# Token numbers stored as three packets of 512 bytes; six raw chunks loaded ahead instead of four

## The chip, the cores and the metric

The kernel runs on one core of a Trainium2 chip. The metric is the device time of one execution, in microseconds (us). Engines: TensorE (PE: matmuls, PEld: weight loads), VectorE (DVE), ScalarE (ACT), GpSimd (POOL), and SyncE (SP), whose queue issues almost all DMAs here.

## The reference

Three stages follow each other. Attention over 2 batches, 8 heads, 768 positions and 64 columns a head, with a band of +-15 positions and 24 block summaries:

```python
mask_l = np.abs(pos[:, None] - pos[None, :]) < window          # window 16
scores_s = scale * np.einsum('bhsd,bhnd->bhsn', q, k_sum) + np.log(block)
a = softmax(concat([where(mask_l, scores_l, -1e9), scores_s]))
x = (a @ concat([v, v_sum])).transpose(0, 2, 1, 3).reshape(1536, 512)
```

A mixture of experts: 8 experts, each token goes to the one with the largest logit, if that one has fewer than 384 tokens yet:

```python
expert_idx = np.argmax(x @ w_gate, axis=1)
h = np.maximum(np.einsum('ecd,edf->ecf', disp, w1), 0.0)        # f = 1024
out[i] = gate_w[i] * y[expert_idx[i], pos[i]] if keep[i] else 0
```

And a dense layer with an ELU: `h = x @ w_in` (2048 columns), `g = where(h > 0, h, exp(min(h, 0)) - 1)`, `out = g @ w_out`. `w_in` and `w_out` come as float64.

## The kernel before

**Attention** runs tile by tile (12 tiles of 128 tokens, two groups of heads each). The gate of each tile finds its tokens' experts and places, and an indirect DMA writes each token's row to `xdisp` in device memory: 512 scaled values and the token's number (in columns 512 to 515).

**Units.** A unit is 384 rows of one expert. Its `load_rows` fetches the rows to `XROW` (128 partitions, 3 tokens in each), `split_x` transposes them and splits them into a high and a low part (`xh`, `xl`: the kernel multiplies float32 in three products), `layer1` and `layer2` are the expert's products, `evict` stores the result to `ydT`. The first unit (`first_unit`) is woven into the end of the attention by hand (`POINTS`, `fill_pe`); the others follow in nested branches, up to 12 in the program. With this input three units run: the first, unit 1 and unit 2 (16 activations of line 1119 are two units of eight). Then three **groups** of 384 rows go through the dense layer, and indirect DMAs write the output by the tokens' numbers.

**Token numbers.** The rows' numbers must come back at the end. `take_ids` (GpSimd) copies them from the rows to `IT`, one per partition and third; `put_ids` (SP, line 1044) stores `IT` to `ids` in device memory: 3 x 128 numbers, each 4 bytes from a partition of its own, thus 384 packets. `load_y` (line 1186) later loads 384 of them the other way, in packets of 4 bytes too.

**Raw chunks.** `w_in` and `w_out` are loaded as 32 chunks of 512 KB and converted from float64 to float32 by three VectorE instructions each (lines 390, 393, 384). Chunks 0 to 15 are `w_in`, 16 to 31 `w_out`. Four chunks (`AHEAD`, 8 to 11) are loaded near the end of the attention to rows 4 to 11 of `wout`, where its keys stood. The others share a ring of three buffers `RAW`: when chunk i of the ring has been converted, `conv_next` issues the load of the third one after it. Conversions 0 to 10 stand in the attention, 11 and 12 in the first unit, 13 to 20 in unit 1, 21 to 28 in unit 2, 29 to 31 in the first group. Rows 12 to 15 of `wout` hold two of the three `VXS` buffers (values of a tile) until the last tile.

**What sets the order.** The schedule is manual: each engine works through its instructions in the order written. SP's queue is in order too: a load that must wait for its buffer holds back all that are written behind it. All of SP's DMAs share one queue on 16 DMA engines.

Of the kernel before, what the change touches and what calls it, by code (L numbers as in the profile page):

```python
# [13 lines left out]
U32 = mybir.dt.uint32  # L14
# [37 lines left out]
def _consts():  # L52
    import numpy as np

    cols = []

    def add(name, a):
        full = np.zeros((P, a.shape[1]), np.float32)
        full[: a.shape[0]] = a
        CONST_COLS[name] = (sum(c.shape[1] for c in cols), a.shape[1])  # L60
        cols.append(full)

    p = np.arange(P)
    add("ident", np.eye(P, dtype=np.float32))
    q = p[:, None] % TQ
    n = np.arange(WK)[None, :]
    band = np.abs(n - WIN - q) < WIN
    first = band & (n >= WIN)
    last = band & (n < WIN + TQ)
    for name, ok in (("mid", band), ("first", first), ("last", last)):  # L70
        m = np.zeros((P, NK), np.float32)
        half = (p[:, None] < TQ) == (name == "first")
        m[:, :WK] = np.where(np.where(half, ok, band), 0.0, NEG)
        add(name, m)

    parts, rest = [], np.float32(8.0 * math.log(BLK))
    for _ in range(3):
        parts.append((np.array([rest]).view(np.uint32) & np.uint32(0xFFFF0000)).view(np.float32)[0])
        rest = np.float32(rest - parts[-1])
    m = np.zeros((P, NB), np.float32)  # L80
    for r in (0, D):
        m[r : r + 3] = np.array(parts, np.float32)[:, None]
    add("logs", m)
    m = np.zeros((P, NK), np.float32)
    m[p[: S // 8], WK + p[: S // 8] // (BLK // 8)] = 1.0 / BLK
    add("means", m)
    add("tri", (p[:, None] < p[None, :]).astype(np.float32))
    add("rev8", np.broadcast_to(E - np.arange(E, dtype=np.float32), (P, E)))
    u = np.arange(NU)
    e, c = u // NCH, u % NCH  # L90

    add("row0", np.repeat(p[:, None] == 0, NU, 1).astype(np.float32))
    add("e_row", np.broadcast_to(e.astype(np.float32), (NU, NU)))
    add("m_row", np.broadcast_to(-NCH * (e + 1.0), (NU, NU)).astype(np.float32))
    add("k_row", np.broadcast_to(NCH * e + 0.0, (NU, NU)).astype(np.float32))
    add("c_row", np.broadcast_to(c + 0.0, (NU, NU)).astype(np.float32))
    add("iota_u", np.broadcast_to(1 + np.arange(MAXU, dtype=np.float32), (NU, MAXU)))
    add("uconst", np.stack([SLOT * c, e, e * REG + SLOT * c - E * REG, e * REG, c >= 0, c == 0, SLOT * (c + 1), -NCH * (e + 1), NCH * e + c], 1).astype(np.float32))
    offsets = np.zeros((1, NLIST * MAXU), np.float32)
    offsets[:, MAXU : 2 * MAXU] = E * REG  # L100
    add("offsets", offsets)
    add("groups", SLOT * np.arange(NG, dtype=np.float32)[None, :])
    tok = (P * np.arange(NTT)[None, :] + p[:, None]).astype(np.int32)
    add("tok", tok.view(np.float32))
    fill = np.zeros((P, 4), np.int32)
    fill[:] = OOB
    add("oob", fill.view(np.float32))
    return np.ascontiguousarray(np.concatenate(cols, axis=1))


# [1 line left out]
def moe_chain_kernel(  # L112
# [83 lines left out]
    WA = [[wp.tile([P, KD, 2 * P], F32R, name=f"wa{w}{n}") for w in "hl"] for n in range(2)]  # L196
    WB = [[wp.tile([P, 2, DM], F32R, name=f"wb{w}{n}") for w in "hl"] for n in range(2)]
    HH = [[wp.tile([P, SLOT], F32R, name=f"h{w}{n}") for w in "hl"] for n in range(3)]
    IT = [cp.tile([P, NS], U32, name=f"it{n}") for n in range(2)]

    def load_w(e, parts, queue=nc.sync):
        for m in parts:
# [43 lines left out]
                )  # L246
            yield

    def split_x(xrow, hps):

        xh, xl = XS1
        for kk in range(KD):
            xp = hps[kk % len(hps)][:, 0:SLOT]
            for s in range(NS):
                nc.tensor.transpose(xp[:, s * P : (s + 1) * P], xrow[:, s, kk * P : (kk + 1) * P], ident)
            nc.scalar.copy(xh[:, kk, :], xp)
            nc.vector.tensor_tensor(xl[:, kk, :], xp, xh[:, kk, :].bitcast(F32), op=ALU.subtract)  # L257
            yield
# [24 lines left out]
    def first_unit():  # L283

        hps = [BANK[7], BANK[0]]
        yield from split_x(XROW0, hps)
        for f in range(F // P):
            hp = hps[f % 2][:, 0:SLOT]
            yield from layer1(hp, WA[f // 2 % 2], f % 2, XS1)
            nc.scalar.activation(HF0[f], hp, AF.Relu)  # L290
            if f % 2 and f // 2 + 2 < F // 256:
                split_a(f // 2 + 2, W1_RAW[f // 2 + 2])
            if f in B_AFTER:
                n = B_AFTER.index(f)
                split_b(WB[n], W2_RAW[n])
            if f in H_AFTER:
                n = H_AFTER.index(f)
                split_h(HH[n], n)
        yield "second"
        for f in range(NF1):  # L300
            yield from layer2(f, HH[f % 4], WB[f // 2 % 2])
            if f == 1:
                split_b(WB[0], W2_RAW[2])
            if f == 3:
                split_b(WB[1], W2_RAW[3])
            while len(HH) < 4:
                yield
            if f + 3 < NF1:
                split_h(HH[(f + 3) % 4], f + 3)
            held["f"] = f  # L310
# [35 lines left out]
    RAW = [wp.tile([P, CE], I64, name=f"raw{n}") for n in range(3)]  # L346


    AHEAD = range(8, 12)
    RING = [i for i in range(NCHUNK) if i not in AHEAD]  # L350

    def raw(i):
# [53 lines left out]
    with ExitStack() as att:  # L406
# [211 lines left out]
        def gate_3(i):  # L618
            gp = GPS[:, i % 2, :]
            lg = gp[:, 0:E]  # L620
            nc.tensor.transpose(lg, st.pop(("g2", i)), C("ident", E)[:, 0:E])
            xr = a3.tile([P, ROW], F32, tag="xr", name="xr")
            o, _ = CONST_COLS["tok"]
            nc.gpsimd.tensor_copy(
                xr[:, DM:].bitcast(U32), cst[:, o + i : o + i + 1].bitcast(U32).to_broadcast([P, ROW - DM])
            )
            mxl, r, nmx, s = sm("mxl"), sm("r") if i else r0, sm("nmx"), sm("s")
            vv, el = sm("vv", E), sm("el", E)
            nc.vector.tensor_reduce(mxl, lg, axis=AX.X, op=ALU.max)
            en = nc.vector if i >= last - 1 else nc.gpsimd  # L630
            en.tensor_scalar(nmx, mxl, -1.0, None, op0=ALU.mult)
            nc.vector.scalar_tensor_tensor(vv, lg, mxl, rev8, op0=ALU.is_ge, op1=ALU.mult)
            nc.vector.tensor_reduce(r, vv, axis=AX.X, op=ALU.max)
            oh = a2.tile([P, E], BF16, tag="oh", name="oh")
            nc.vector.tensor_scalar(oh, rev8, r, None, op0=ALU.is_equal)
            if i >= last - 1:
                nc.scalar.activation(el, lg, AF.Exp, bias=nmx, accum_out=s)
                st["g4", i] = (None, xr, s)
            if i == 0:
                ohs[0] = oh  # L640
            else:
                ohs[i] = oh_x if i == X_TILE else a3.tile([P, E], BF16, tag="ohsum", name="ohsum")
                en.tensor_tensor(ohs[i], ohs[i - 1], oh, op=ALU.add)
            st["g3", i] = (gp, oh, r, s, el, nmx, xr)
# [129 lines left out]
        def late(n):  # L774
# [10 lines left out]
                nc.vector.memset(ones_f, 1.0)  # L785
            if n == 1:
                nc.gpsimd.memset(fill_row, 0.0)
                nc.gpsimd.tensor_copy(fill_row[:, DM:].bitcast(U32), C("oob").bitcast(U32))
                nc.gpsimd.tensor_copy(oobs, C("oob")[:, 0:1].bitcast(U32).to_broadcast([P, REG // P]))  # L789
                nc.vector.tensor_copy(cap, cap_raw.bitcast(I32)[:, 0:1])  # L790
            if n in (2, 4):
                load_k(1, n - 2, 2)
# [34 lines left out]
                for m in range(len(RAW)):  # L827
                    conv_load(m)
            if n == NST - 2:
                for m in AHEAD:  # L830
                    conv_load(m)
            if n >= CONV_FROM and conv[0] < CONV_ATT and n % 2 == 0:
                pieces.extend(conversion(conv[0]))
# [82 lines left out]
        for gate, *at in tail:  # L916
            gate(*at)
            if gate is rest_o and at[1]:
                held["acc"] = False
            point()  # L920


# [114 lines left out]
    def expert_of(j, queue=nc.sync):  # L1037
        return queue.value_load(listed(0, j), min_val=0, max_val=E - 1)

    def take_ids(j, xrow):  # L1040
        nc.gpsimd.tensor_copy(IT[j % 2], xrow[:, :, DM].bitcast(U32))

    def put_ids(j, base, queue=nc.sync):
        queue.dma_start(ids[ds(base, SLOT), :].rearrange("(s p) o -> p s o", p=P), IT[j % 2].unsqueeze(2))

    def prologue(n):

        if n == 0:
            split_a(0, W1_RAW[0])
        elif n == 1:  # L1050
            for _ in split_x(XROW, HP):
                pass

    def branch_ahead(label, hint):
# [4 lines left out]
    def rest_of_first():  # L1059

        while not held["second"]:
            fill_pe(1)
        take_ids(0, XROW0)
        expert = expert_of(1)
        load_w(expert, range(2))
        load_x(1)
# [3 lines left out]
        while done < NF1 - 1:  # L1070

            while done < held["f"]:
# [3 lines left out]
                if done in CONV_FIRST:  # L1076
                    convert(CONVS[0] + CONV_FIRST.index(done))
                if done in PROLOGUE:
                    prologue(PROLOGUE.index(done))
                if done == HINT_FIRST:  # L1080
                    n_units = nc.values_load(listed(NLIST - 1, 0), min_val=0, max_val=MAXU)
                    branch_ahead("units0", n_units > 1)
# [14 lines left out]
    def unit(j, expert, finish):  # L1097

        if j > 1:
            load_w(expert, NEXT[2])  # L1100
            for n in range(2):
                prologue(n)
        base = nc.sync.value_load(listed(2, j), min_val=0, max_val=NT)
        if j + 1 < MAXU:
            branch_ahead(f"units{j}", n_units > j + 1)
        take_ids(j, XROW)
        put_ids(j, base)
        if j + 1 < MAXU:
            load_x(j + 1)
# [294 lines left out]
```

## Time and profile before

| | us |
|---|---|
| median of 3 runs | 448.73 (444.07, 448.73, 449.82) |
| the profiled execution | 448.12 |
| its span, first to last instruction | 446.4 |
| TensorE busy | 418.7 (94%) |
| VectorE busy | 344.6 (77%) |
| ScalarE busy | 234.0 (52%) |
| GpSimd busy | 71.0 (16%) |
| DMA queue of SP | 58.16 MB, 44.8% of 16 engines |

Up to 141 us attention and gate run, with parts of the first unit; the units to 235 us, the groups from there. The page cuts the span into 40 slices of 11.16 us; a digit is the busy share in tenths. The busy share of the whole span is a mean over stages with different limits; which engine another one waits for is read from the timelines of a stage. In a timeline a row gives start and duration, and in brackets the idle time of the engine before it with what ended that. `SPq` rows are issues of DMAs, not the transfers.

### The profile page before, as it was taken

Reading aid. Unit: us, or ns where it says so; the run is one execution under the profiler, and the core shown is the slowest. Engines: PE = TensorE matmul, PEld = TensorE weight load, DVE = VectorE, ACT = ScalarE, POOL = GpSimd, SP = SyncE. Lnnn points to the kernel's source line nnn. Section 1 sums busy time; section 2 is a strip of 40 time slices with the busy share of each in tenths; the row PEclk is TensorE's granted clock in tenths of the full one; section 3 lists DMA queues with packets and bytes.
Section 4 is the critical chain, followed back from the end, with each engine's and each line's share of the span. In section 5 each row is a group of like instructions: output and inputs, shape, how many; then the busy total and the mean of one; then the engine's idle time right before and its main releaser. Section 6 shows DMA issues by size and latency. Waiting matters only on the chain.

```text
span 446.4 us, 8022 instructions
## 1 busy us (share of the span) xinstructions
PE 418.7 (94%) x2759; PEld 360.5 (81%) x2759; DVE 344.6 (77%) x763; ACT 234.0 (52%) x581; POOL 71.0 (16%) x138
## 2 busy tenths in 40 slices
PE   7899999996887999789999999999999999999994
PEld 3567767774777999679998888788998988998983
DVE  4555998977675955979598999999777877777871
ACT  3364778884453565146347677754444334444331
POOL 2201685965311000000000000000200000200002
PEclk9967999998999999899999999999999999999999
DMA  8968799979501999889856900020100020100001
GB/s 271 245 183 270 249 322 287 282 220 292 214 0 34 188 288 204 280 277 147 310 187 220 346 6 1 0 73 0 72 1 1 0 71 1 71 1 0 1 3 71
DMA packets 33779, 63.50 MB, mean 142 GB/s; under 512 B 5877, under 2 KB 16117, under 8 KB 33728
## 3 DMA queue, kind: packets, MB, share of 16 engines
q1 hardware_dynamic: 32048, 58.16, 44.8%
q0 software_dynamic: 1680, 4.74, 2.8%
q8 instruction: 23, 0.38, 0.3%
q14 instruction: 28, 0.23, 0.2%
HBM read 50.26 MB, written 13.42 MB: 143 GB/s over the span
## 4 chain that ended last, share of the span: by engine, by line
PE 32%; issue 31%; DVE 19%; DMA 8%; ACT 5%; POOL 3%; SPq 1%; another core or an unknown queue 0%; POOLq 0%; DVEq 0%; ACTq 0%
PE bank L244 10%; PE bank L264 10%; PE bank L1232 3%; DMA raw<-in_moe_w_out_dram 3%; DMA w2raw<-in_v_dram 2%; PE bank L524 2%; PE bank L613 2%; DMA ydT<-ysb 2%; PE bank L576 2%; DMA cap_raw<-in_moe_capacity_dram 1%; DVE wout_r L1212 1%; PE bank L565 1%; DVE win_r L1212 1%; DVE mx L536 1%; POOL out_dram L1244 1%
## 5 line engine op out<-in xcount | busy, mean ns | idle before, releaser
L1232 PE MATMUL bank<-wout_r,hh 128*128 128x512 f32 x144 | 57.3, 398 | 1.5 <-DVE wout_r L1212 1.5
L548 ACT ACTIVATE ex<-bank,nm 128x120 f32<-128x120 f32 x96 | 33.6, 365 | 7.9 <-DVE nm L541 4.5
L1232 PEld LDWEIGHTS bank<-wout_r,hh 128*128 128x128 f32 x144 | 27.0, 188 | 7.3 <-DVE wout_r L1212 2.8
L1280 ACT ACTIVATE hf<-bank 128x384 f32<-128x384 f32 x24 | 11.8, 491 | 38.9 <-PE bank L244 38.9
L1280 ACT ACTIVATE xrow<-bank 128x384 f32<-128x384 f32 x24 | 11.8, 490 | 38.1 <-PE bank L244 38.1
L1232 PE MATMUL bank<-w2raw_r,hl 128*128 128x512 f32 x72 | 28.7, 399 | 0.0
L1232 PE MATMUL bank<-w2raw_r,hh 128*128 128x512 f32 x72 | 28.3, 393 | 0.0
L524 PE MATMUL bank<-spare,qt 64*64 64x120 f32 x384 | 26.7, 282 | 1.5 <-DMA qt<-in_q_dram 1.5
L244 PE MATMUL bank<-xh,wal 128*128 128x384 f32 x112 | 25.1, 346 | 3.1 <-DVE wal L237 3.1
L244 PE MATMUL bank<-yh,win_r 128*128 128x384 f32 x128 | 26.8, 337 | 0.0
L244 PE MATMUL bank<-xh,wah 128*128 128x384 f32 x112 | 24.6, 340 | 2.4 <-DVE xl L257 2.2
L1244 POOL DMA_INDIRECT out_dram<-raw,idt x6 | 6.1, 1023 | 119.8 <-ACT raw L1241 118.6
L244 PE MATMUL bank<-xl,wah 128*128 128x384 f32 x112 | 24.9, 344 | 0.0
L1244 POOL DMA_INDIRECT out_dram<-ysb,idt x3 | 2.9, 975 | 137.7 <-DVE xrow L1296 137.1
L524 PEld LDWEIGHTS bank<-spare,qt 64*64 64x64 f32 x384 | 21.0, 141 | 3.0 <-POOL oobs L789 1.2
L244 PEld LDWEIGHTS bank<-xh,wal 128*128 128x128 f32 x112 | 20.0, 192 | 3.9 <-DVE wal L237 3.4
L244 PEld LDWEIGHTS bank<-yh,win_r 128*128 128x128 f32 x128 | 22.7, 188 | 0.4
L244 PEld LDWEIGHTS bank<-xh,wah 128*128 128x128 f32 x112 | 19.7, 188 | 3.7 <-DVE xl L257 2.5
L1119 ACT ACTIVATE hf<-bank 128x384 f32<-128x384 f32 x16 | 7.9, 493 | 27.9 <-PE bank L244 27.7
L264 PE MATMUL bank<-hh,wbh 128*128 128x384 f32 x96 | 21.2, 343 | 0.0
L536 DVE TENSOR_REDUCE mx<-bank 128x4 f32<-128x480 f32 x24 | 15.6, 651 | 7.0 <-PE bank L524 6.9
L264 PE MATMUL bank<-hh,wbl 128*128 128x384 f32 x96 | 20.8, 337 | 0.0
(254 smaller groups left out, 1140.6 us busy)
## 6 DMA issues: line engine op xcount, KB each, us to landing
raw<-in_moe_w_out_dram SPq DMA_DIRECT2D x16, 512.0 KB
raw<-in_moe_w_in_dram SPq DMA_DIRECT2D x12, 512.0 KB
w1raw<-in_moe_w_dram SPq DMA_DIRECT2D x12, 512.0 KB
w2raw<-in_moe_w_dram SPq DMA_DIRECT2D x12, 512.0 KB
qt<-in_q_dram SPq DMA_DIRECT2D x12, 256.0 KB
w2raw<-in_v_dram SPq DMA_DIRECT2D x8, 384.0 KB
yr<-ydT SPq DMA_DIRECT2D x4, 768.0 KB
out_dram<-fill_row SPq DMA_DIRECT2D x4, 768.0 KB
```

Source lines behind the costliest of these rows:

```text
L244: nc.tensor.matmul(hp, wa[a][:, kk, cols], xa[b][:, kk, :], start=(n == kk == 0), stop=(n == 2 and kk == KD - 1))
L264: nc.tensor.matmul(ACC[d][:, 0:SLOT], wb[a][:, jj, d * P : (d + 1) * P], hb[b], start=(f == 0 and n == 0), stop=(f == NF1 - 1 and n == 2),)
L524: nc.tensor.matmul(sp[j * TQ : (j + 1) * TQ, u, :], qts[i][rows, u, j * TQ : (j + 1) * TQ], kws[i][rows, u, j, :], start=False, stop=(u == 3),
L536: nc.vector.tensor_reduce(mx, sp, axis=AX.X, op=ALU.max)
L548: nc.scalar.activation(ex[:, u, :], sp[:, u, :], AF.Exp, bias=nm[:, u : u + 1], scale=0.125, accum_out=den[:, u : u + 1])
L576: nc.tensor.matmul(op[j * TQ : (j + 1) * TQ, u, :], es[:, u, j * TQ : (j + 1) * TQ], vx[:, j, (2 * u + g) * D : (2 * u + g + 1) * D], star ...
L613: nc.tensor.matmul(lt, wg[:, kk, :], xT[:, kk, :], start=(kk == 0), stop=(kk == KD - 1))
L1119: nc.scalar.activation(hf, hp, AF.Relu)
L1212: nc.vector.tensor_tensor(lo, src, hi.bitcast(F32), op=ALU.subtract)
L1232: nc.tensor.matmul(ACC[s], ga[a][:, cols], wb[b][:, jj, :], start=(f == n == 0), stop=(f == NF2 - 1 and n == 2),)
L1244: put = nc.gpsimd.indirect_dma_start(out, bass.IndirectOffsetOnAxis(ap=IDT[g % 3][:, s : s + 1], axis=0), OBS[(NS * g + s) % len(OBS)], No ...
L1280: nc.scalar.activation(x, hp, AF.Relu, scale=-1.0)
```

## The change

Token numbers are float values now (`tok`, `oob`), no longer integer bits. `take_ids` on GpSimd is gone. Instead `split_x` begins with a product of the rows' number columns (128 x 3) with the identity, which gives 3 partitions of 128 numbers in a free part of a PSUM bank; ScalarE copies it to `IT`, now 3 x 128, as integers. `put_ids` stores it as three packets of 512 bytes. `AHEAD` holds six chunks: 8 to 11 are loaded where they were, 12 and 13 to rows 12 to 15 of `wout`, issued when the last tile's product with its values has been issued (`rest_o`). The ring loses chunks 12 and 13.

```diff
-    IT = [cp.tile([P, NS], U32, name=f"it{n}") for n in range(2)]
+    IT = [cp.tile([NS, P], U32, name=f"it{n}") for n in range(2)]
...
-    def split_x(xrow, hps):
+    def split_x(xrow, hps, it):
 
         xh, xl = XS1
+        at = hps[0][0:NS, SLOT : SLOT + P]
+        nc.tensor.matmul(at, xrow[:, :, DM], ident, start=True, stop=True)
+        nc.scalar.copy(IT[it], at)
         for kk in range(KD):
...
-    AHEAD = range(8, 12)
+    AHEAD = range(8, 14)
...
-                nc.gpsimd.tensor_copy(oobs, C("oob")[:, 0:1].bitcast(U32).to_broadcast([P, REG // P]))
+                nc.gpsimd.tensor_copy(oobs, C("oob")[:, 0:1].to_broadcast([P, REG // P]))
...
-                for m in AHEAD:
+                for m in AHEAD[:4]:
                     conv_load(m)
...
             if gate is rest_o and at[1]:
                 held["acc"] = False
+                for m in AHEAD[4:]:
+                    conv_load(m)
             point()
...
-    def take_ids(j, xrow):
-        nc.gpsimd.tensor_copy(IT[j % 2], xrow[:, :, DM].bitcast(U32))
-
     def put_ids(j, base, queue=nc.sync):
-        queue.dma_start(ids[ds(base, SLOT), :].rearrange("(s p) o -> p s o", p=P), IT[j % 2].unsqueeze(2))
+        queue.dma_start(ids[ds(base, SLOT), :].rearrange("(s p) o -> s (p o)", p=P), IT[j % 2])
```

SP's queue at the end of the attention, before and after (`rows` is `wout`, `raw_...` the ring; the order numbers the ring's buffers 154 to 156). Before:

```order
L365 DMA raw_154<-in_moe_w_in_dram 128x512
L365 DMA rows<-in_moe_w_in_dram 128x512 x4
L205 ISA
L205 DMA w2raw_136<-in_moe_w_dram 128x2x512
L365 DMA raw_155<-in_moe_w_in_dram 128x512
L1038 TENSOR_LOAD lists_i
```

After:

```order
L365 DMA raw_154<-in_moe_w_in_dram 128x512
L365 DMA rows<-in_moe_w_in_dram 128x512 x4
L202 ISA
L202 DMA w2raw_136<-in_moe_w_dram 128x2x512
L365 DMA raw_155<-in_moe_w_out_dram 128x512
L365 DMA rows<-in_moe_w_in_dram 128x512 x2
L1040 TENSOR_LOAD lists_i
```

The ring's load ahead of the lists was chunk 14 and is now chunk 16, of `w_out`; behind it stand the two new loads (chunks 12 and 13), still ahead of SP's read of the lists.

SP's queue in unit 1, from the store of the first unit's result to unit 2's first weights. Before:

```order
L1154 DMA ydT<-ysb 128x4x384
L365 DMA raw_154<-in_moe_w_out_dram 128x512
L365 DMA raw_155<-in_moe_w_out_dram 128x512
L365 DMA raw_156<-in_moe_w_out_dram 128x512
L365 DMA raw_154<-in_moe_w_out_dram 128x512
L1038 TENSOR_LOAD lists_i
L1038 ISA x2
L1136 TENSOR_LOAD lists_i
L1136 ISA x2
L1137 COMPARE_AND_BRANCH
L209 ISA
L209 DMA w1raw_122<-in_moe_w_dram 128x4x256
```

After:

```order
L1151 DMA ydT<-ysb 128x4x384
L365 DMA raw_156<-in_moe_w_out_dram 128x512
L365 DMA raw_154<-in_moe_w_out_dram 128x512
L365 DMA raw_155<-in_moe_w_out_dram 128x512
L1040 TENSOR_LOAD lists_i
L1040 ISA x2
L1133 TENSOR_LOAD lists_i
L1133 ISA x2
L1134 COMPARE_AND_BRANCH
L206 ISA
L206 DMA w1raw_122<-in_moe_w_dram 128x4x256
```

Four ring loads (chunks 16 to 19) stood ahead of unit 2's weights; now three (17 to 19). Chunk 20's load stands behind the first three weight loads in both.

ScalarE in the prologue of unit 1 (`xh` are the casts of `split_x`), after:

```order
L280 CAST hh_2208<-w1raw_128 128x384
L251 CAST it_153<-bank_92 3x128
L256 CAST xh_93<-bank_92 128x384
L256 CAST xh_93<-bank_85 128x384
L256 CAST xh_93<-bank_90 128x384
L256 CAST xh_93<-bank_91 128x384
```

Only the cast to `it` is new; the others stood in this order before. On TensorE the product stands likewise just ahead of the first transpose.

## Rows read from the trace of the kernel before

**Rows 1.** Page, 40 slices: TensorE's busy tenths, and GB/s of all DMAs

```profile
PE   7899999996887999789999999999999999999994
...
GB/s 271 245 183 270 249 322 287 282 220 292 214 0 34 188 288 204 280 277 147 310 187 220 346 6 1 0 73 0 72 1 1 0 71 1 71 1 0 1 3 71
```

**Rows 2.** Stages: length, busy us of each engine (instructions), granted clock, DMA share, GB/s

```profile
core 0: us, PE busy (x) PEld busy (x) DVE busy (x) ACT busy (x) POOL busy (x), PEclk, DMA share, GB/s
...
179.00:182.30 3.30, 0.18 (x2) 0.02 (x1) 3.02 (x5) 0.00 (x0) 0.00 (x0) 1.00 0.50 180
182.30:186.00 3.70, 3.70 (x12) 3.70 (x13) 3.63 (x6) 0.81 (x2) 0.00 (x0) 0.54 0.79 242
195.00:197.40 2.40, 0.17 (x2) 0.03 (x1) 2.40 (x5) 0.00 (x0) 0.00 (x0) 1.00 0.79 241
197.40:235.00 37.60, 37.60 (x216) 37.47 (x217) 30.53 (x48) 17.56 (x29) 0.00 (x0) 1.00 0.80 224
```

**Rows 3.** Timeline of TensorE: the two matmuls behind a gap, with what released them

```profile
182.28 1.56 PE L244 MATMUL bank<-xh,wal 128*128 128x384 f32 x4 [3.12 <-DVE wal L237]
...
197.37 0.98 PE L244 MATMUL bank<-xh,wah 128*128 128x384 f32 x4 [2.23 <-DVE xl L257]
```

**Rows 4.** Timeline of VectorE, units 1 and 2: first instructions of chunks 16, 17, 20, 24; `xl`

```profile
179.21 0.43 DVE L390 TENSOR_SCALAR wout<-raw 128x512 uint32<-128x512 uint32 x1 [5.53 <-DMA raw<-in_moe_w_out_dram]
...
182.61 0.42 DVE L390 TENSOR_SCALAR wout<-raw 128x512 uint32<-128x512 uint32 x1
...
191.76 0.43 DVE L390 TENSOR_SCALAR wout<-raw 128x512 uint32<-128x512 uint32 x1 [1.63 <-DMA raw<-in_moe_w_out_dram]
...
196.30 1.94 DVE L257 TENSOR_TENSOR xl<-bank,xh 128x384 fp32r<-128x384 f32 x4
...
217.64 0.43 DVE L390 TENSOR_SCALAR wout<-raw 128x512 uint32<-128x512 uint32 x1 [4.35 <-DMA raw<-in_moe_w_out_dram]
```

**Rows 5.** Stages of the DMA: around the stores of numbers, and two others

```profile
34.00:36.00 2.00, 2.00 (x19) 1.70 (x16) 0.31 (x1) 0.31 (x1) 0.00 (x0) 0.50 1.03 369
145.00:149.00 4.00, 4.00 (x24) 4.00 (x24) 3.93 (x7) 2.83 (x4) 0.00 (x0) 1.00 1.03 344
149.00:159.00 10.00, 10.00 (x63) 9.97 (x63) 7.15 (x12) 3.51 (x7) 0.35 (x1) 1.00 0.85 99
...
167.00:175.00 8.00, 8.00 (x48) 8.00 (x47) 6.55 (x10) 4.70 (x8) 0.00 (x0) 1.00 1.00 117
204.00:212.00 8.00, 8.00 (x48) 8.00 (x47) 7.19 (x13) 6.47 (x11) 0.00 (x0) 1.00 0.91 57
246.00:250.00 4.00, 4.00 (x22) 3.63 (x21) 3.86 (x8) 2.53 (x5) 0.00 (x0) 1.00 1.01 285
```

**Rows 6.** Timeline of SP: issues of stores to `ids`, a load from it, a ring load

```profile
29.42 0.38 SPq L794 DMA_DIRECT2D ids<-oobs  x1
...
115.71 0.33 SPq L365 DMA_DIRECT2D raw<-in_moe_w_in_dram  x1
...
147.20 0.41 SPq L1044 DMA_DIRECT2D ids<-it  x1
...
162.29 0.41 SPq L1044 DMA_DIRECT2D ids<-it  x1
...
201.99 0.41 SPq L1044 DMA_DIRECT2D ids<-it  x1
...
245.39 0.39 SPq L1186 DMA_DIRECT2D idt<-ids  x1
```

**Rows 7.** Chain of waits: chunk 16, start and length

```profile
167.83 11.28 DMA raw<-in_moe_w_out_dram
```

**Rows 8.** The ring's tile `raw`: its loads, from issue to landing

```profile
DMA to landing us min/median/max: 2.7/2.7/3.6
```

**Rows 9.** Timeline of TensorE: twelve transposes of unit 1

```profile
152.67 1.47 PE L255 MATMUL bank<-cst,xrow 128*128 128x128 f32 x12
```

**Rows 10.** Timeline of ScalarE: a small copy from PSUM

```profile
126.10 0.26 ACT L615 COPY ls<-bank 8x128 f32<-8x128 f32 x1 [0.82 <-PE bank L613]
```

More of the change, by code (lines that the diff above doesn't have):

```diff
@@ L102, in _consts @@
     add("groups", SLOT * np.arange(NG, dtype=np.float32)[None, :])
[L103 to L107, printed above, removed]
+    add("tok", (P * np.arange(NTT)[None, :] + p[:, None]).astype(np.float32))
+    add("oob", np.full((P, 4), OOB, np.float32))
     return np.ascontiguousarray(np.concatenate(cols, axis=1))
@@ L285, in first_unit @@
         hps = [BANK[7], BANK[0]]
-        yield from split_x(XROW0, hps)
+        yield from split_x(XROW0, hps, 0)
         for f in range(F // P):
@@ L624, in gate_3 @@
             nc.gpsimd.tensor_copy(
-                xr[:, DM:].bitcast(U32), cst[:, o + i : o + i + 1].bitcast(U32).to_broadcast([P, ROW - DM])
+                xr[:, DM:], cst[:, o + i : o + i + 1].to_broadcast([P, ROW - DM])
             )
@@ L787, in late @@
                 nc.gpsimd.memset(fill_row, 0.0)
-                nc.gpsimd.tensor_copy(fill_row[:, DM:].bitcast(U32), C("oob").bitcast(U32))
-                nc.gpsimd.tensor_copy(oobs, C("oob")[:, 0:1].bitcast(U32).to_broadcast([P, REG // P]))
+                nc.gpsimd.tensor_copy(fill_row[:, DM:], C("oob"))
+                nc.gpsimd.tensor_copy(oobs, C("oob")[:, 0:1].to_broadcast([P, REG // P]))
                 nc.vector.tensor_copy(cap, cap_raw.bitcast(I32)[:, 0:1])
@@ L1038, in expert_of, with prologue @@
         return queue.value_load(listed(0, j), min_val=0, max_val=E - 1)
-    def take_ids(j, xrow):
-        nc.gpsimd.tensor_copy(IT[j % 2], xrow[:, :, DM].bitcast(U32))
     def put_ids(j, base, queue=nc.sync):
-        queue.dma_start(ids[ds(base, SLOT), :].rearrange("(s p) o -> p s o", p=P), IT[j % 2].unsqueeze(2))
-    def prologue(n):
+        queue.dma_start(ids[ds(base, SLOT), :].rearrange("(s p) o -> s (p o)", p=P), IT[j % 2])
+    def prologue(j, n):
         if n == 0:
@@ L1050, in prologue @@
         elif n == 1:
-            for _ in split_x(XROW, HP):
+            for _ in split_x(XROW, HP, j % 2):
                 pass
@@ L1062, in rest_of_first @@
             fill_pe(1)
-        take_ids(0, XROW0)
         expert = expert_of(1)
@@ L1078, in rest_of_first @@
                 if done in PROLOGUE:
-                    prologue(PROLOGUE.index(done))
+                    prologue(1, PROLOGUE.index(done))
                 if done == HINT_FIRST:
@@ L1101, in unit @@
             for n in range(2):
-                prologue(n)
+                prologue(j, n)
         base = nc.sync.value_load(listed(2, j), min_val=0, max_val=NT)
@@ L1105, in unit @@
             branch_ahead(f"units{j}", n_units > j + 1)
-        take_ids(j, XROW)
         put_ids(j, base)
```

## The prediction

> **What bounds the kernel now.** I read the page's slices first [rows 1], 11.16 us each, counted from 0. From slice 13 (145 us) on TensorE is busy 90% or more, but for slices 16 and 17 (178.6 to 200.9 us: 0.7 and 0.8); and GB/s, which is near 280 around them, is only 188, 204 and 147 in slices 13, 15 and 18. So I asked for stages. [...]
>
> What ends the gaps? The first matmul behind the first one waited for `wal` of line 237, the one behind the second for `xl` of line 257, both VectorE's [rows 3]. On VectorE one reads why they were late [rows 4]: it sat 5.53 us until chunk 16, the first of `w_out`, had landed, and began its conversion at 179.21, ahead of `wal`. It waited once more, 1.63 us, for chunk 20, and `xl` began at 196.30. In unit 2 it waits a third time, 4.35 us, for chunk 24; there TensorE goes on without a gap [rows 2].
>
> Why is a load of 512 KB so slow? The DMA stages tell [rows 5]. After each of the three stores of token numbers (line 1044, issued at 147.20, 162.29 and 201.99 us [rows 6]) the engines stay 85 to 100% busy and yet move 99, 117 and 57 GB/s, for 10, 8 and 8 us, against 344 in the stretch ahead of the first. Such a store is 384 packets of 4 bytes. It is the store and not what comes with it: that stretch at 344 holds most of the first unit's `xrow` rows, which were issued ahead of the store; behind the 4-byte load of line 1186 (issued at 245.39) 285 are left; and the store of `oobs` (128 packets of 60 bytes, issued at 29.42) is followed by 369 at 34 to 36 us. Chunk 16 was issued at 167.83, behind the second store and three `xrow` loads, and stands with 11.28 us in the chain of waits [rows 7].
>
> **The change, part by part.** I count against the profiled execution: 448.12 us, its span 446.4, 0.6 under the median of the runs (448.73).
>
> (1) *The store becomes three packets of 512 bytes.* Before has none such. From below: the 60-byte packets cost nothing that is seen. From above: each packet at the price of a 4-byte one, 3/384 of 10 us, 0.1 us. I take 0; the slow stretches go.
>
> (2) *Chunks 12 and 13 go to places that the attention leaves.* The ring's chunks shift: where SP issued chunks 12, 13 and 14 it issues 14, 15 and 16. Chunk 15's and chunk 16's loads leave the busy time after 147 us, and two loads are added behind the last attention product. Chunk 16 takes the place of the load at 115.71 and has landed at 118.4, by the usual 2.7 us from issue to landing [rows 6, 8]. The two new loads run into a slice without bytes (slice 11, from 122.8 us: 0 GB/s [rows 1]), and their chunks are wanted in units 0 and 1, behind 145 us; without that cover they cost 2.7 us each. From chunk 17 on the loads run three ahead, as they did.
>
> (3) *What the vanished wait is worth.* VectorE is free at 179.21 - 5.53 = 173.68. Chunk 16 starts there: 5.5 us earlier. What is late next? Chunk 17, which VectorE reaches 3.4 us later (179.21 to 182.61 [rows 4]), at 177.1. Its load waits for the end of chunk 14, by that pace near 169 us; in an undisturbed queue it lands at 172. No wait; chunk 18 likewise. Chunk 19's load waits for the end of chunk 16, and behind it on SP stand unit 2's first weight loads and chunk 20's, as the rows of SP's order show: all of these move by the same 5.5 us, in the same order, so I keep chunk 20's wait of 1.63 us. Then `xl` starts at 190.8 instead of 196.30 and the matmul of 197.37 at 191.9. Is TensorE there by then? The product that it stood before at 182.28 follows at 178.99 (182.28 less 3.3, by the stage); up to that matmul there are 14 steps of four matmuls, 0.70 us each (216 in 37.6 us [rows 2]), the transposes (1.47) and the new product (0.1): 190.4. It still idles 1.5 us, and VectorE's chain is what counts: gain 5.5 us. What the low clock cost lies inside, since TensorE then waits anyway. Behind 197.4 TensorE is gapless, so the gain stays 5.5: the 4.35 us of chunk 24 are worth nothing more.
>
> (4) *The new product and copy.* One of each per unit, three units here. Transposes of the same 128 columns take 1.47 us for 12, 0.12 each; ScalarE's copy of 8x128 from PSUM 0.26 [rows 9, 10]. In the first unit both stand ahead of the first `xh`, on the way to an `xl` that the attention's own VectorE work queues behind: from 0 (ScalarE waits there) to 0.1 + 0.26. I take 0.3. In unit 1 (slices 13 to 15) TensorE is gapless: 0.1. In unit 2 both fall into its idle time: 0. GpSimd loses three copies that nothing waits for but the store; the store now waits for ScalarE's copy, next to the transposes at 152.67, and SP comes to it at 162.29: no new wait, and the loads queued behind it keep their places. `oobs` becomes a conversion on GpSimd, off every chain: 0.
>
> Sum: 448.12 - 5.5 + 0.3 + 0.1 = **443.0 us**, 1.3% under the median.
>
> **The rivals.**
> *Chunk 20 does not wait either.* With the queue clean its load may come the 1.6 us earlier; TensorE starts unit 2 at 190.4, when it can: 441.5. Against it: its queue mates move with it, and the second store was no longer in the way there. Chance 0.22.
> *The slow stretch stays* (it comes of storing to `ids` at all, or of the `xrow` loads). Then chunk 17 stands where chunk 16 stood and lands at 179.2; VectorE, there at 177.1, loses 2.1 of the 5.5: 448.12 - 3.4 + 0.4 = 445.1. Against it: the 60-byte store and the first `xrow` rows. 0.10.
> *The stall moves undiminished to chunk 17.* The ring still feeds it only three ahead. If it lands behind 177.1 + 5.5 = 182.6, nothing is gained, and product and copy are paid: 448.12 + 0.4 = 448.5, slower than before. For it: a load issued a little earlier took 11 us. Against it: even so, chunk 17 was converted at 182.61 without a wait [rows 4]. 0.08.
> *The clock falls in the gap that is left.* 3.3 us of idling were followed by 0.54 of the clock, 2.4 us were not [rows 2], so 1.5 us should not be. If it does, I take the stage from 182.3 to 186: 3.7 us at 0.54 do what 2.0 do at full clock, 1.7 lost: 444.7. [...] 0.08.
>
> **How the numbers follow.** My forecast has 0.52, the rivals in their order 0.22, 0.10, 0.08 and 0.08. From 440.0 to 446.5 lie all but the stall that moves, 0.92; I leave a tenth more at the edges for a median that is not the profiled execution (the three runs lie between 444.07 and 449.82). Two per cent, about what a measurement of this kernel can tell from no change, is 9.0 us. Faster than 439.8 is what the runs' spread makes of the first rival (a third of it) and of my own case (a tenth): 0.13. Slower than 457.7 is none of them; 0.03 for what I do not see. The rest, 0.84, is within 2%.
>
> **What would show it.** Right: no stretch under 200 GB/s behind a store of line 1043 while loads are pending; no VectorE wait for chunk 16; TensorE at full clock at 182 us and its first product of unit 2 near 191.9; two chunk loads in the slices that were empty. Wrong: VectorE waiting for chunk 17 or 18; TensorE idle longer than before ahead of 141 us; 57 to 117 GB/s behind the new stores; or a gain behind 197.4 us, where I expect none.

## The result and the profile after

| | us |
|---|---|
| kernel before, median of 20 runs | 449.68 (443.85 to 460.32) |
| changed kernel, median of 20 runs | 445.56 (439.59 to 453.34) |
| ratio changed / before, with its 95% interval | 0.9887 [0.985, 0.9924] |

The ratio is that of the faster executions of each kernel, so it is not the quotient of the two medians (0.9908). By the ratio the changed kernel takes 1.1% less: 5.1 us of 449.68, within two per cent. Put on the 448.12 us of the profiled execution before, that is 443.1, with an interval from 441.4 to 444.7; the forecast was 443.0, from 440.0 to 446.5. The lines below are from a second profile of the changed kernel (441.28 us, span 439.4), with a mean granted clock of 0.95 up to the routing (0.89 in the first).

The page's slices, 10.99 us each (TensorE's busy tenths, its granted clock in tenths, GB/s):

```profile
PE   7899899988987999999999999999999999999994
...
PEclk9999999995899999999999999999999999999999
...
GB/s 281 263 224 256 313 319 287 274 208 334 179 36 17 326 260 100 320 289 245 222 150 211 291 1 0 1 72 1 73 0 1 0 74 0 73 0 0 1 2 74
```

From slice 13 on TensorE is at 90% or more, but for the last slice: the 0.7 and 0.8 of slices 16 and 17 [rows 1] are gone, and slice 11, which was empty, carries bytes. The stages of the DMA tell more; the first three begin some 2 us behind each of the three stores:

```profile
147.00:155.00 8.00, 7.66 (x49) 7.11 (x48) 7.46 (x13) 3.76 (x8) 0.00 (x0) 1.00 1.00 321
157.00:165.00 8.00, 8.00 (x48) 8.00 (x47) 5.12 (x8) 5.67 (x9) 0.00 (x0) 1.00 0.71 218
197.00:205.00 8.00, 8.00 (x47) 8.00 (x47) 7.19 (x13) 6.27 (x11) 0.00 (x0) 1.00 0.75 205
190.65:192.65 2.00, 2.00 (x11) 2.00 (x12) 2.00 (x3) 0.00 (x0) 0.00 (x0) 1.00 0.99 297
```

321, 218 and 205 GB/s stand where 99, 117 and 57 stood [rows 5]. In the second and third the engines are only 71 and 75% busy: the queue is short of work there. The second pair does not compare like with like, since the stretch of [rows 5] began 5 us behind its store; from 2 us on, the kernel before moves 199 GB/s there. VectorE's timeline, the first instructions of chunks 16 and 17, then of chunk 20:

```profile
172.71 0.42 DVE L390 TENSOR_SCALAR wout<-raw 128x512 uint32<-128x512 uint32 x1
...
176.10 0.42 DVE L390 TENSOR_SCALAR wout<-raw 128x512 uint32<-128x512 uint32 x1
...
185.04 0.43 DVE L390 TENSOR_SCALAR wout<-raw 128x512 uint32<-128x512 uint32 x1 [1.41 <-DMA raw<-in_moe_w_out_dram]
```

Neither chunk 16 nor 17 is waited for; chunk 20 still is, 1.41 us after 1.63 [rows 4]. On TensorE the product that stood 3.12 us [rows 3] follows at once (178.12), and unit 2's first product stands 0.39 us instead of 2.23. What is new is a wait of the transposes:

```profile
178.12 0.85 PE L241 MATMUL bank<-xh,wal 128*128 128x384 f32 x4
...
185.89 0.38 PE L250 MATMUL bank<-cst,xrow 128*3 128x128 f32 x2
186.62 1.53 PE L255 MATMUL bank<-cst,xrow 128*128 128x128 f32 x12 [0.34 <-ACT it L251]
...
190.65 0.96 PE L241 MATMUL bank<-xh,wah 128*128 128x384 f32 x4 [0.39 <-DVE xl L257]
```

**A ruler.** Up to the routing the same program takes 140.8 to 149.9 us in the executions below, which is more than anything that is to be compared. The two extremes had a mean granted clock of 0.95 and 0.86 up to there; the clock is not all of it, since 140.98 and 144.60 us both stand at 0.93. So I measure from SP's first weight load of unit 1, issued right behind its read of the lists (142.60 before), to unit 2's first product, and on to the end of the span. In the timeline of SP, the kernel before:

```profile
142.60 0.40 SPq L209 DMA_DIRECT2D w1raw<-in_moe_w_dram  x1
```

and the changed kernel, with the loads of chunks 16, 12 and 13 ahead of it:

```profile
113.42 0.33 SPq L365 DMA_DIRECT2D raw<-in_moe_w_out_dram  x1
113.86 5.53 SPq L365 DMA_DIRECT2D rows<-in_moe_w_in_dram  x2
140.82 0.40 SPq L206 DMA_DIRECT2D w1raw<-in_moe_w_dram  x1
```

Each row is one profiled execution; (a) lists to unit 2's first product, (b) from there to the end, both in us:

| kernel | (a) | TensorE idle ahead of that product | (b) | (a)+(b) | ratio to before |
|---|---|---|---|---|---|
| before | 54.77 | 2.23 (and 3.12 earlier) | 249.03 | 303.80 | |
| changed | 49.83 | 0.39 | 248.75 | 298.58 | 0.9887 [0.985, 0.9924] |
| ids_only | 49.78 | 0.34 | 248.72 | 298.50 | 0.9822 [0.9778, 0.9867] |
| chunks_only | 50.47 | 2.83 | 250.49 | 300.96 | 0.9883 [0.9825, 0.9942] |
| pitch64 | 50.35 | 2.71 | 250.32 | 300.67 | 0.9881 [0.9797, 0.9965] |
| pitch64_chunks | 50.45 | 2.81 | 250.45 | 300.90 | none |
| bank_only | 49.51 | 0.75 | 248.74 | 298.25 | 0.9923 [0.987, 0.9977] |
| conv_later | 49.24 | none | 248.56 | 297.80 | 0.9833 [0.9788, 0.9879] |
| bank_conv | 48.58 | none | 248.62 | 297.20 | 0.9805 [0.9752, 0.9858] |
| pitch64_conv | 47.47 | none | 248.75 | 296.22 | 0.981 [0.9759, 0.9861] |
| pitch8 / pitch16 / wide32 | 49.99 / 49.64 / 50.13 | 2.37 / 2.00 / 2.49 | 250.17 / 250.42 / 250.38 | 300.16 / 300.06 / 300.51 | one run each |

Before to changed: 4.94 us in (a) and 0.28 in (b), 5.2 together, which the ratio's 5.1 agrees with. The first profile of the changed kernel gives 299.07. So differences of up to half a microsecond in this table are no more than the scatter of one kernel. Of the kernel before there is one profile. The ratios hardly separate the kernels of the table.

### The profile page after: what moved, and what is told of

Its sections match the earlier page's. It is cut to its first block, busy times and chain, and to the rows that moved or that the text cites. A ratio compares the mean times of both kernels' runs of the same rounds, so it can differ in the third digit from the quotient of the medians.

```text
span 444.5 us, 8028 instructions
## 1 busy us (share of the span) xinstructions
PE 423.7 (95%) x2765; PEld 363.9 (82%) x2765; DVE 346.6 (78%) x763; ACT 234.2 (53%) x584; POOL 69.2 (16%) x135
## 4 chain that ended last, share of the span: by engine, by line
PE 37%; issue 31%; DVE 14%; DMA 9%; ACT 4%; POOL 3%; SPq 1%; another core or an unknown queue 0%; POOLq 0%; DVEq 0%; ACTq 0%
PE bank L241 11%; PE bank L264 9%; PE bank L524 3%; PE bank L1229 3%; PE bank L576 2%; DMA raw<-in_moe_w_in_dram 2%; PE bank L565 2%; DMA w2raw<-in_v_dram 2%; PE bank L613 2%; DMA ydT<-ysb 2%; DMA raw<-in_moe_w_out_dram 2%; DVE wout_r L1209 1%; DVE win_r L1209 1%; DMA cap_raw<-in_moe_capacity_dram 1%; POOL out_dram L1241 1%
## 5 line engine op out<-in xcount | busy, mean ns | idle before, releaser
L1277 ACT ACTIVATE hf<-bank 128x384 f32<-128x384 f32 x24 | 11.8, 491 | 39.0 <-PE bank L241 39.0
L241 PE MATMUL bank<-xh,wah 128*128 128x384 f32 x112 | 25.7, 352 | 1.1 <-DVE xl L257 0.9
L264 PE MATMUL bank<-hl,wbh 128*128 128x384 f32 x96 | 20.6, 336 | 0.0
L1292 DVE SCALAR_TENSOR_TENSOR xrow<-hf,xrow 128x384 f32<-128x384 f32 x24 | 13.3, 556 | 9.3 <-ACT hf L1279 9.3
```

The costliest lines, as they stand in the source:

```text
L241: nc.tensor.matmul(hp, wa[a][:, kk, cols], xa[b][:, kk, :], start=(n == kk == 0), stop=(n == 2 and kk == KD - 1))
L264: nc.tensor.matmul(ACC[d][:, 0:SLOT], wb[a][:, jj, d * P : (d + 1) * P], hb[b], start=(f == 0 and n == 0), stop=(f == NF1 - 1 and n == 2),)
L1277: nc.scalar.activation(x, hp, AF.Relu, scale=-1.0)
L1292: nc.vector.scalar_tensor_tensor(z, x, 1.0, z, op0=ALU.add, op1=ALU.mult)
```

## The experiments

**The changed kernel again** (`again`).

> The changed kernel once more, for a profile of it at an undisturbed clock. My theory: TensorE has no gap near 182 us and full clock there; VectorE waits for no chunk up to 19, and 1.6 to 1.9 us for chunk 20; unit 2's first product comes near 191.9 us, 5.5 us earlier than before, and behind it nothing more is gained: about 443 us. Rival (the gain came from ahead of 145 us): the span from SP's read of the lists to the end is as long as before.

444.6 us, ratio 0.9899 [0.9827, 0.9972]. Its lines stand above: no gap near 182, chunk 20 waited for by 1.41 us, the first product 4.94 us earlier by the ruler. The rival falls: the gain lies behind the lists.

**The store alone** (`ids_only`).

```diff
-    AHEAD = range(8, 14)
+    AHEAD = range(8, 12)
```

> Only the store of three packets with its product and copy; four chunks ahead as before. My theory: the two parts of the change do the same work twice. With the queue clean, chunk 16, issued near 167.8 us as before, lands 3 to 4 us later, before VectorE comes to it at 173.7: no wait, no gap in TensorE, 448.1 - 5.5 + 0.4 = 443.0 us, as with the whole change. Rival A (the chunks that were moved carry the gain): VectorE still waits for chunk 16 by several us, about 448 us. Rival B (half and half): chunk 16 waits 2 to 3 us, about 445.5 us.

444.65 us. VectorE takes chunk 16 without a wait and waits 1.37 us for chunk 20; 298.50 us by the ruler against 298.58. The store by itself gives all that the ruler shows; the two chunks add nothing to it. Rivals A and B fall.

**The chunks alone** (`chunks_only`: the kernel before, with `AHEAD` as changed).

```diff
-    AHEAD = range(8, 12)
+    AHEAD = range(8, 14)
...
-                for m in AHEAD:
+                for m in AHEAD[:4]:
...
+                for m in AHEAD[4:]:
+                    conv_load(m)
```

> Only the six chunks; the store of 384 packets of 4 bytes stays. My theory: the stretches at 57 to 117 GB/s behind the stores stay; chunk 16 has long landed; chunk 17 stands where chunk 16 stood and lands near 179.2 us, VectorE is there at 177.1 and waits 2.1 us: 448.1 - 3.4 = 444.7 us. Rival A (the ring absorbs it): no wait for chunk 17, 442.6 us. Rival B (the stall moves undiminished): chunk 17 waits 5 us or more, 448 us.

446.32 us, ratio 0.9883. The stages first (behind the first store, then before and after unit 2's first product), then VectorE at chunk 17 and TensorE at that product:

```profile
149.00:157.00 8.00, 8.00 (x52) 7.97 (x51) 7.08 (x12) 3.50 (x7) 0.69 (x1) 1.00 0.97 96
...
190.00:193.00 3.00, 0.17 (x1) 0.00 (x0) 3.00 (x6) 0.00 (x0) 0.00 (x0) 1.00 0.78 208
193.01:195.01 2.00, 2.00 (x7) 2.00 (x8) 2.00 (x3) 0.00 (x0) 0.00 (x0) 0.54 0.95 321
195.01:197.01 2.00, 2.00 (x9) 2.00 (x8) 0.00 (x1) 0.05 (x1) 0.00 (x0) 0.61 1.05 369
```

```profile
178.85 0.43 DVE L390 TENSOR_SCALAR wout<-raw 128x512 uint32<-128x512 uint32 x1 [1.85 <-DMA raw<-in_moe_w_out_dram]
```

```profile
193.01 1.53 PE L244 MATMUL bank<-xh,wah 128*128 128x384 f32 x4 [2.83 <-DVE xl L257]
```

Slow stretch and wait are as the theory had them: 96 GB/s, 1.85 us for chunk 17 where 2.1 were expected. What it did not have is the rest: TensorE idles 2.83 us ahead of unit 2's first product, and then its granted clock is 0.54 and 0.61 of full. Four matmuls that take 0.85 us take 1.53. It costs 1.7 us in (b) (250.49 to 248.75). Even so the chunks alone are worth 2.8 us by the ruler (303.80 to 300.96), with the slow stretches still there.

**The same packets, each in a place of its own** (`pitch64`: the kernel before, 64 bytes from number to number; the edits below, and the first fill of `ids` and its read-back made to fit).

```diff
-    ids = dram.tile([REG, 1], U32, name="ids")
+    ids = dram.tile([REG, 16], U32, name="ids")
...
-        queue.dma_start(ids[ds(base, SLOT), :].rearrange("(s p) o -> p s o", p=P), IT[j % 2].unsqueeze(2))
+        queue.dma_start(ids[ds(base, SLOT), 0:1].rearrange("(s p) o -> p s o", p=P), IT[j % 2].unsqueeze(2))
```

> The kernel before, with each token number stored 64 bytes from the next: still 384 packets of 4 bytes per store, but no two of them within the same 64 bytes; the lists are read back at the same pitch, which makes that load 4-byte packets at 64-byte steps. If the number of the packets makes the stretches slow, 57 to 117 GB/s stay for 8 to 10 us behind each store, VectorE waits 5.5 us for chunk 16, 448 us. If it is that neighbouring packets write into the same place in memory, the stretches go (over 250 GB/s), chunk 16 is not waited for, and the time is near 443 us.

445.35 us. Behind the three stores:

```profile
149.00:157.00 8.00, 8.00 (x53) 7.97 (x52) 6.71 (x11) 3.51 (x7) 1.26 (x1) 1.00 0.98 326
159.00:167.00 8.00, 8.00 (x48) 8.00 (x47) 6.46 (x11) 7.15 (x12) 0.98 (x1) 1.00 0.95 279
199.00:207.00 8.00, 8.00 (x48) 8.00 (x47) 7.17 (x13) 5.00 (x9) 0.00 (x0) 1.00 0.85 268
```

Still 384 packets of 4 bytes per store, and the slow stretches are gone, chunk 16's wait with them. Neither the number nor the size of the packets alone made the queue slow; it is that they were written close together. The same 4-byte packets cost the queue nothing visible once they lay apart: 326, 279 and 268 GB/s.

**How near is too near** (`pitch16`, `pitch8`: the same edit with 16 and 8 bytes; `wide32`: packets of 32 bytes that adjoin, made by GpSimd's copy). The first lines of the edit of `pitch8`, whose rest is that of `pitch64`, and the two main edits of `wide32`, which stores eight copies of each number:

```diff
-    ids = dram.tile([REG, 1], U32, name="ids")
+    ids = dram.tile([REG, 2], U32, name="ids")
```

```diff
-    IT = [cp.tile([P, NS], U32, name=f"it{n}") for n in range(2)]
+    IT = [cp.tile([P, NS, 8], U32, name=f"it{n}") for n in range(2)]
...
-        nc.gpsimd.tensor_copy(IT[j % 2], xrow[:, :, DM].bitcast(U32))
+        nc.gpsimd.tensor_copy(IT[j % 2], xrow[:, :, DM : DM + 1].bitcast(U32).to_broadcast([P, NS, 8]))
```

> The kernel before with 16 bytes from one token number to the next, so that four packets of 4 bytes lie in 64 bytes instead of sixteen, over 6 KB instead of 1.5 KB. If the packets hold each other up in proportion to how many of them share a place of 64 bytes, the slow stretch behind a store is some 2.5 us instead of 10, and chunk 16 is waited for hardly or not. If any sharing costs the full price, the 8 to 10 us at 57 to 117 GB/s stay.

> The kernel before with 8 bytes from one token number to the next: eight packets of 4 bytes in 64 bytes, over 3 KB. With 16 bytes (four packets) a dip of some 4 us at 80 GB/s was left behind the third store only, with 4 bytes (sixteen) 8 to 10 us behind each. If the price rises step by step with the number that share a place, this lies between: dips of 3 to 6 us, chunk 16 waited for by 0 to 3 us. If there is an edge between four and sixteen, it looks like one of the two.

> The kernel before with each token number stored eight times, as one packet of 32 bytes that adjoins the next: 384 packets per store still, two of them in 64 bytes, over 12 KB with no bytes left out. [...] If sharing a place is what costs, this is as clean as the pitch of 16 bytes or cleaner, chunk 16 is not waited for, and SP's read of the lists to the end takes about 300 us (303.8 before, 300.1 and 300.7 with the pitches of 16 and 64). If packets that adjoin without a gap are what costs, 57 to 117 GB/s for 8 to 10 us stay.

444.87, 444.97 and 444.9 us, one execution each. The table counts, in the traces, packets of 1 KB or more that took over 1 us within 14 us of each of the three stores, and gives GB/s in the 8 us that begin about 2 us behind the first and the third:

| distance (packet) | packets in 64 bytes | slow packets | GB/s |
|---|---|---|---|
| 4 (4): before | 16 | 33, 31, 38 | 97, 57 |
| 8 (4) | 8 | 10, 7, 15 | 293, 219 |
| 16 (4) | 4 | 6, 5, 9 | 289, 237 |
| 32 (32) | 2 | 1, 1, 10 | 315, 216 |
| 64 (4) | 1 | 3, 5, 1 | 326, 268 |
| changed: 512 (512) | | 2, 1, 6 | 321, 205 |

It is the loads' own packets that get slow, and the price rises steeply only between eight and sixteen packets in 64 bytes: for a price that rises step by step I had expected dips of 3 to 6 us at eight, and one such dip is left, behind the third store (200 to 204 us: 38 GB/s, engines 64% busy). A stretch at 78 GB/s that is left with 16 bytes (199.4 to 203.4) is no clear dip: the engines are 42% busy there. Packets of 32 bytes that adjoin are no slower than these: adjoining as such is not the cause. Whether it counts how many share a place or how small the whole region is (1.5 KB before, 3, 6, 12 and 24 in the order of the rows) these runs do not tell: both change together.

**The changed kernel without its product** (`pitch64_chunks`: the diffs of `chunks_only` and of `pitch64` together).

> The changed kernel without its product and copy: six chunks ahead, and the old store with 64 bytes between the numbers, which leaves the queue as clean. My theory: the product and copy cost TensorE 0.9 us per unit, but they fill a gap that VectorE leaves anyway, and so the clock does not fall behind it. Without them TensorE idles 2.0 to 2.8 us ahead of unit 2's first product instead of 0.4, its granted clock falls to 0.5 to 0.7 for some 4 us, and SP's read of the lists to the end takes 300.0 to 300.7 us instead of 298.6: taking work out makes it 1.4 to 2.1 us slower. Rival (product and copy are a cost like any other): 298.6 less some tenths, up to 1.8 us less.

The four executions lie between 444.29 and 451.58 us, too far apart for a ratio. The ruler gives 300.90 us, the stages around unit 2's first product:

```profile
192.20:195.05 2.85, 0.04 (x2) 0.00 (x1) 2.85 (x6) 0.00 (x0) 0.00 (x0) 1.00 0.87 221
195.05:197.05 2.00, 2.00 (x7) 2.00 (x8) 2.00 (x3) 0.00 (x0) 0.00 (x0) 0.56 0.89 299
197.05:199.05 2.00, 2.00 (x9) 2.00 (x8) 0.00 (x1) 0.05 (x1) 0.00 (x0) 0.59 1.08 367
```

As the theory has it: 2.81 us idle, a clock of 0.56 and 0.59, and 2.3 us more than with the product and copy (the stores differ too, but the queue is as clean: 3, 2 and 0 slow packets by the count above). 1.7 of them are in (b), the clock; 0.6 in (a), where chunk 20 lands later (VectorE waits 2.93 us for it). Some 0.9 us of that longer wait are VectorE coming sooner to chunk 20; why the chunk itself lands 0.6 us later is open.

**Product in the other bank** (`bank_only`), and with chunk 20 moved to unit 2 (`conv_later` alone, `bank_conv` with both, `pitch64_conv` on the kernel before with the pitch).

```diff
-        at = hps[0][0:NS, SLOT : SLOT + P]
+        at = hps[1][0:NS, SLOT : SLOT + P]
...
-    CONV_UNIT = (2, 8, 8)
+    CONV_UNIT = (2, 7, 9)
```

> The changed kernel with the product in the other bank, so that the transposes don't wait 0.34 us for its copy; chunk 20 stays in unit 1. My theory: TensorE comes 0.7 us earlier to the gap ahead of unit 2's first product, which VectorE ends, so the gap grows from 0.4 to some 1.0 us; that is too short for the clock to fall (0.91 us were not followed by a fall, 2.0 were), and the time from SP's read of the lists to the end stays at 298.6 within 0.3 us. Rival (the clock falls behind 1.0 us too): 300 us.

443.59 us. The gap grows to 0.75 us where 1.0 was expected, the clock stays (the first three steps of four matmuls behind the gap take 0.97, 0.88 and 0.85 us), 298.25 by the ruler. Of the 0.7 us that TensorE saves in two units it idles 0.36; the other 0.3 are within the scatter of the ruler.

> The changed kernel with chunk 20 converted at the start of unit 2 (seven chunks in unit 1 and nine in unit 2, for eight and eight), so that xl of unit 2 no longer stands behind the wait for it. In the profile of the changed kernel at an undisturbed clock, VectorE waits 1.41 us for chunk 20 and converts it in 1.9 us, and TensorE idles only 0.39 us ahead of unit 2's first product. My theory: TensorE's own work, longer by 0.9 us per unit through the new product, its copy and the 0.34 us that the transposes wait for the copy, is now the limit there; the 3.3 us of VectorE are worth 0.4 us, which these rounds hardly tell from nothing. Rival (VectorE is still the limit): 1.4 us or more gained over the changed kernel.

442.21 us. By the ruler 297.80, 0.8 less than the changed kernel where 0.4 were expected, and not the 1.4 or more of the rival.

> As the run before it, and the new product goes to the other of the two banks that the transposes fill, so that the first transposes don't wait for its copy. My theory: the wait of 0.34 us goes in units 1 and 2, unit 2's first product comes some 48.7 us after SP's read of the lists (49.8 in the changed kernel), 1.1 us gained over the changed kernel. Rival: the second group of transposes waits in its place and nothing is gained over the run before.

441.74 us. TensorE around the transposes:

```profile
194.61 0.39 PE L250 MATMUL bank<-cst,xrow 128*3 128x128 f32 x2
194.92 1.62 PE L255 MATMUL bank<-cst,xrow 128*128 128x128 f32 x12
```

The wait of 0.34 us is gone, and nothing waits in its place: 0.6 less again, 0.3 per unit.

> The kernel before with 64 bytes between the token numbers, as in the run of that change alone, and chunk 20 converted in unit 2; no new product. With the pitch alone TensorE idled 2.71 us for xl of unit 2 and then ran three steps of four matmuls at 1.08 to 1.65 us instead of 0.85, since its granted clock fell behind that gap. My theory: the gap goes, and the low clock with it; unit 2's first product comes 47.5 us after SP's read of the lists (50.35 with the pitch alone, 49.8 in the changed kernel), and from there to the end it is 248.7 us instead of 250.3: 4.4 us less than with the pitch alone, 2.4 less than the changed kernel, about 441 where the kernel before is at 449. Rival (the fall of the clock does not hang on the gap): only 2.7 us less than with the pitch alone. Rival (nine conversions in unit 2 make VectorE late there): nothing gained.

440.14 us, ratio 0.981 [0.9759, 0.9861]: it beats the kernel before by 1.9% with the lowest median of all, though its interval overlaps those of the two before it and touches the changed kernel's. TensorE at unit 2's first product, without a gap, and the stages from there:

```profile
188.45 0.85 PE L244 MATMUL bank<-xh,wah 128*128 128x384 f32 x4
```

```profile
188.45:190.45 2.00, 2.00 (x13) 2.00 (x13) 0.96 (x1) 0.00 (x0) 0.00 (x0) 1.00 0.95 326
190.45:192.45 2.00, 2.00 (x14) 2.00 (x13) 0.65 (x2) 1.69 (x3) 0.00 (x0) 1.00 1.08 399
```

47.47 and 248.75 us where 47.5 and 248.7 were expected: without the gap the clock does not fall, and moving chunk 20 is worth 4.4 us over the pitch alone. Both rivals fall. Beside `conv_later` (49.24), where TensorE waits for nothing but the copy, it also prices the product and its copy: 1.77 us of TensorE in two units, 0.9 in each, 0.3 of it the wait for the copy. The stores and the chunks of the two kernels differ too, so the price is read once more below, from TensorE's rows alone.

## Why the prediction was right, step by step

The time came out, but by the time alone the forecast (443.0) cannot be told from two of its rivals (441.5 and 444.7), which stand in the same interval. The lines tell them apart. Two errors in the forecast lay where they cost nothing.

**Where TensorE was bound** held: both gaps (3.12 and 2.23 us [rows 3]) were VectorE's, VectorE's were chunk 16 and 20, and chunk 16's delay was the store's. The tell, engines 85 to 100% busy at 57 to 117 GB/s right behind three stores, pointed at the store rightly. *Why* the store is slow was put down to its being 384 packets of 4 bytes; the pitch shows that lying close together is part of it (97 GB/s behind the first store, 326 with 64 bytes between the numbers).

**(1) Three packets cost nothing**: right (321 GB/s behind them).

**(2) Two chunks more ahead**: right in that nothing new waits. Of the two loads only the second runs into the stretch that was empty (121 to 123 us: 164 GB/s); the first, issued at 113.86, runs ahead of it, beside other loads. But the step hid that the two halves of the change do the same work. The forecast gave chunk 16's wait to both at once; `ids_only` shows that the store alone gives it, `chunks_only` that the chunks alone take it away too, and with it 2.8 of the 5.2 us, though VectorE then loses 1.85 us to chunk 17. On top of a clean queue (`pitch64_chunks` beside `pitch64`, the changed kernel beside `ids_only`) they add nothing measurable.

**(3) 5.5 us, rigidly**: chunk 16's wait went, 17 to 19 had none, chunk 20's stayed at 1.41 us for 1.63. By the ruler the product of unit 2 came 4.94 us earlier; 5.4 were forecast (5.5 less 0.1). The half microsecond is the next step's: VectorE waits longer for TensorE's results at 158 us (3.61 us ahead of `ysb`, 3.03 before), and comes to chunk 16 31.9 us after the lists instead of 31.1. Of these 0.8 us it gets 0.2 back at chunk 20: 5.53 - 0.81 + 0.22 = 4.94.

**(4) Product and copy** is the term that was wrong in size: 0.1 us in unit 1 and 0 in unit 2 were taken, from transposes and a copy apart; it is 0.9 in each. TensorE's rows show it in unit 2, from the last step ahead of the transposes to the first behind them, 1.93 us in the kernel before and 2.80 in the changed one:

```profile
190.88 0.86 PE L264 MATMUL bank<-hl,wbh 128*128 128x384 f32 x4
...
192.81 0.94 PE L264 MATMUL bank<-hh,wbh 128*128 128x384 f32 x4
```

```profile
185.10 0.86 PE L264 MATMUL bank<-hl,wbh 128*128 128x384 f32 x4
...
187.90 0.96 PE L264 MATMUL bank<-hh,wbh 128*128 128x384 f32 x4
```

I added the durations and left out that the product's bank is also that of the first transposes, and that TensorE could wait there for ScalarE's copy in between; in the changed kernel it does, 0.34 us. And I took a twelfth of a row of transposes for the price of one product: from its start to the first transpose 0.73 us pass, and still 0.31 in `bank_conv`, without the wait. The last 0.15 us are in the rows beside it. In `bank_only` and `bank_conv`, with the product in the other bank, the wait is gone: the transposes follow 0.32 and 0.31 us behind the product's start. The first unit's 0.3 us cannot be seen: that part varies by 9 us from run to run.

That 1.8 us of unforeseen TensorE work did not cost 1.8 us is the gap's doing. The forecast had TensorE idle 1.5 us ahead of unit 2; with the real price it idles 0.39. So the size was wrong and the sum was not, and that is luck: the unforeseen work filled a gap that, left open, is followed by a fall of the clock in the runs without the product (to 0.50 to 0.76).

**The rivals.** *Chunk 20 does not wait*: no. *The slow stretch stays*: `chunks_only` is that case, and the forecast of it held at chunk 17 (1.85 us for 2.1). *The stall moves undiminished*: no. *The clock falls in the gap that is left* got 0.08, because one gap of 2.23 us had not been followed by a fall. That reading was too thin: in six kernels without the product 2.00 to 2.83 us of idling were each followed by a fall to between 0.50 and 0.76. Had the product cost 0.1 us as forecast, the gap would by my estimate have been some 2 us (0.39 and the 1.7 us too little) and this rival likely. Why the 2.23 us of the kernel before were not followed by a fall is open, and with one profile of it so is whether they never are. *No gain behind 197.4*: 0.28 us, about the scatter.

**The sum again.** A clean queue without the product is worth 3.1 us by the ruler (303.80 to 300.67), the changed kernel 5.2. Of the other 2.1, 1.6 are the clock in (b) (250.32 to 248.75), which does not fall (1.00) where the product and its copy fill the gap; 0.5 are in (a), where chunk 20 lands later without the product, and their cause is open. Moving chunk 20 takes the gap away from the other side and is worth more (7.6 us, `pitch64_conv`).

## What to carry to other kernels

When a queue is busy and moves few bytes, ask what was written just ahead of the stretch, and whether many tiny writes land next to each other; spreading them apart takes a few lines (97 GB/s behind the first store became 326 here). Price a new instruction by its place, not by its duration: who reads its bank, and who needs that bank next (0.34 us here, none in the other bank). And before counting a shortened wait in full, see what gap is left for TensorE, since behind gaps of 2.0 to 2.8 us the clock cost another 1.4 to 1.7 us here; where single runs scatter more than the effect, measure from an event behind the noise.

## What the runs showed of the hardware

Behind the three stores of the kernel before (sixteen 4-byte writes in 64 bytes) the queue moved 57 to 117 GB/s for 8 to 10 us; with eight one dip of 4 us was left behind the third store (38 GB/s), with four and with one none that is clear. The delay was on the loads' packets: 33, 31 and 38 of them took over 1 us, against 3, 5 and 1 with one write in 64 bytes. The runs with eight and four are one execution each.

TensorE's granted clock: 2.00, 2.37, 2.49, 2.71, 2.81 and 2.83 us of idling were followed by 0.50 to 0.76 over the next two stretches of 2 us; 0.34, 0.39, 0.75 and 0.91 us were not, nor was the 2.23 us of the kernel before [rows 2]. Why 2.00 us was followed by a fall and 2.23 was not, no run here shows. In the six kernels with a fall the rest of the span, (b), is 1.4 to 1.7 us longer than in the changed kernel.

The stretch up to the routing, in which TensorE idles 13.4 and 12.3 us in the two extremes, took 140.8 and 149.9 us there, at a mean granted clock of 0.95 and 0.86.
